# Keys of two groups in one turning DMA, x of the last two groups and z in fewer, heads a call later, and outputs stored behind the next load of u

## The chip, the cores and the metric

One core of a Trainium2 chip. The time is that of the whole kernel on the device, in microseconds; lower is better. Three runs of the kernel before gave 765.2, 765.59 and 769.08 us, median 765.59.

## The reference

Eight batches of 3200 tokens with 256 features. An attention without softmax, gated by `u`, gives `x`; a token mixer follows.

```python
scores = (1/S) * (z @ z.T)                # z: 3200 x 64, so scores are symmetric
x      = u * (maximum(scores, 0)**2 @ v)  # 3200 x 256
wq, wk = x @ w_q, x @ w_k                 # 3200 x 64 each
W_tok  = (1/8) * (wq @ wk.T)
out    = maximum(W_tok @ x, 0) @ w_out
```

The kernel never forms `W_tok`. It builds `wk.T @ x` (64 x 256, called the heads), multiplies that with `wq` (the mix), applies the maximum, and multiplies with `w_out` (the projection to the output).

## The kernel before

The 3200 tokens of a batch are 25 tiles of 128, in six groups of 512 and a last one of 128 (LASTG, the short group). Groups are worked off one after the other, batch after batch, in phases counted by `k`. The loop `while groups` (lines 1012 to 1215) writes out one phase per turn, and each engine gets its instructions in that written order; no planner reorders them.

A usual phase holds three pairs of score tiles (`scores`, L291) and a share of the second product (`acc`, L353) of the current group. A pair of score tiles is two matmuls that use 64 rows of TensorE each and run side by side, 512 columns long. The first stage takes the maximum (`g`, on DVE L305 or ACT L303), the second squares it (`at`, on POOL L316 or ACT L314). Two phases later `at` is the weight of the second product, with `v` as the moving side. Since the scores are symmetric, some `at` tiles are also turned by a DMA on SP's queue (`tt`, `ts`, L335) and serve a later group.

The second product is issued in two lanes: the upper 64 rows work on one bank of the accumulator and the lower 64 on the other (`first_pass`), then they change banks (`second_pass`). `swap_after` puts a wait for the first pass's last matmuls between them. Score pairs of the phase are placed at shares of it given by `shares_of` (L932), or, for the first `heading` of them (L1039 to L1045), ahead of everything:

```python
heading = len(pairs)
if on_lanes:
    heading = heading - 2 * bool(keying or projecting) if begins else 1 - bool(mixing)
```

So a phase that begins a group and holds neither a key call nor a projection has all its pairs ahead.

When a group closes, `gate` reads the two accumulator banks: DVE multiplies one with `u` (`x_sb`, L491), ACT copies the other (`gt`, L490) and POOL multiplies that (L493). The accumulator has one buffer per half, so the next group's first `acc` waits for both reads. `turn_x` turns x by a DMA (L502). Some phases later a key call (`keys_and_heads`, `k` below) projects a group: a matmul gives 64 rows of `wq` and 64 of `wk` in one PSUM tile `qk`. ACT copies all 128 rows to `qk` in SBUF (L528), and `turn_keys` turns the key half by a DMA (L535). The same call holds the heads of an earlier group, two key calls back, which DVE adds up (`ha`, L578). With the last group, DVE writes `hT` (L582) and TensorE turns it through the identity (`turn_heads`, L594). Then come six mix pieces a batch (`mix`, `m` below: two matmuls, one `rt` on ACT, and two score pairs instead of three) and six projections (`project`, `p` below: 16 `fo` matmuls, one ACT scaling L723, a store L724 on SP's queue at once). The short group's mix and projection ride along in key calls as side items.

Which phase holds a `k`, `m` or `p` is decided by rules (`mix_due`, `key_due`, `projecting`), with exceptions for 15 phases in `chosen` (L895). PSUM holds three two-bank tiles (`pps`), shared by scores, `qk`, `mx` and `fo`, and two accumulator banks. The last batch and the ending (a list of words, L82) are written out by hand.

Of the kernel before, what the change touches and what calls it, by code (L numbers as in the profile page):

```python
# [16 lines left out]
def kernel(  # L17
# [170 lines left out]
    zeros = consts.tile([P, P], FP16, tag="zeros", name="zeros")  # L188
    kxs = [pk.tile([P, 4, 2, dh], FP16, tag=f"kx{i}", name=f"kx{i}") for i in range(4)]
    raw = {}  # L190

# [27 lines left out]
    LASTG = NG - 1  # L219

    def is_turned(gi, gj):
        return gi < gj < LASTG and (gj <= gi + FAR or (gi, gj) == (0, 4))

    FOR_SMALL = (3, 4, 5)

# [244 lines left out]
    def gate(b, gi):  # L472
        nn = widths[gi] // P
        if gi < LASTG:
            xs[b, gi] = px.tile([P, 4, D], FP16, tag="x_sb", name="x_sb")
        else:
            xs[b, gi] = px.tile([P, 1, D], FP16, tag="xl", name="xl", bufs=1)
        x = xs[b, gi][:].rearrange("p n d -> p (n d)")
        ug = us.pop((b, gi))[:].rearrange("p n d -> p (n d)")
# [16 lines left out]
    def turn_x(b, gi):  # L496
        nn = widths[gi] // P
        if gi < LASTG:
            xTs[b, gi] = pxt.tile([P, 4, ND, P], FP16, tag="xT_sb", name="xT_sb")
        else:  # L500
            xTs[b, gi] = pxt.tile([P, 1, ND, P], FP16, tag="xTl", name="xTl", bufs=1)
        nc.sync.dma_start_transpose(  # L502
            out=xTs[b, gi][:, 0:nn, :, :].rearrange("p n a s -> p (n a) s"),
            in_=xs[b, gi][:, 0:nn, :].rearrange("p n d -> p (n d)"),
        )


# [14 lines left out]
    def projections_out(b, gi, out):  # L522
        gw = widths[gi]
        if gi < LASTG:
            qks[b, gi] = pq.tile([P, W], FP16, tag="qk", name="qk")
        else:
            qks[b, gi] = pq.tile([P, P], FP16, tag="ql", name="ql", bufs=2)
        nc.scalar.copy(out=qks[b, gi][:, 0:gw], in_=out)  # L528

    def turn_keys(b, gi):  # L530
        gw = widths[gi]
        mine = slice(0, dh) if swapped(gi) else slice(dh, P)
        kxs.append(kxs.pop(0))
        ks[b, gi] = kxs[-1]
# [170 lines left out]
    def proj_out(b, gi, src, ways):  # L705

        n0 = starts[gi] // P
        if groups:
            fo = pfo.tile([P, 2, W], FP32, tag="fo", name="fo")
        else:  # L710
            fo = pg.tile([P, 2, W], FP32, tag="g", name="fo")
        flat_out = fo[:].rearrange("p a w -> p (a w)")
        at = 0
        for on_dve, queue, n in ways:
            sl = slice(at * D, (at + n) * D)
            part = src[at // 2][:, 0 : n * D] if isinstance(src, list) else src[:, sl]
# [7 lines left out]
            queue.dma_start(  # L724
                out=rows(out, b)[:, n0 + at : n0 + at + n, :],
                in_=flat_out[:, sl].rearrange("p (n d) -> p n d", d=D),
            )
            at += n

# [34 lines left out]
    def side_proj_out(b, ps):  # L764
        fo = pfo.tile([P, D], FP32, tag="fs", name="fs", bufs=1)
        nc.scalar.mul(out=fo[:], in_=ps[:, 1, D : 2 * D], mul=FINAL_SCALE)
        nc.sync.dma_start(out=rows(out, b)[:, NT - 1, :], in_=fo[:])


    fillers = []  # L770
    to_load = []
    todo_mix, todo_proj, todo_between, at_phase, side = [], [], [], {}, []
    keyed, keyed_at, to_turn, to_spread, asides = [], [-9], [], [], []
    hTs, to_turn_heads = {}, []

# [6 lines left out]
    def group_done(k, b, gi):  # L782
        if gi < LASTG - 1:
            between(k + (5 if b + 1 < B else 3), lambda: keys_and_heads(b, [gi]))
        elif gi == LASTG and b + 1 < B:
# [11 lines left out]
    def keys_and_heads(b, gis):  # L797
# [5 lines left out]
        aside = None  # L803
        late = len(groups) <= NG
        heads_of = keyed[: late or len(keyed) == 2]
        if late and len(keyed) == 2 and keyed[0][0] == keyed[1][0]:
            heads_of = [(keyed[0][0], keyed[0][1] + keyed[1][1])]
            keyed[:2] = heads_of
        full = len(heads_of) == 1
        if full:  # L810
# [7 lines left out]
            if heads_of[0][0] < last and more < D:  # L818
# [5 lines left out]
                banks[1][-1].stop = False  # L824
                banks[1] += projections(b, gis[0], w, ps[:, 1, 0:P], start=False, n0=W // P - 1)
        assert full or len(gis) == 1
        if full and heads_of[0][0] < last and heads_of[0][1][-1] == LASTG:
# [4 lines left out]
        def after():  # L832
# [3 lines left out]
            if full:  # L836
                hb, hgis = keyed.pop(0)
                heads_out(hb, hgis, ps)
# [4 lines left out]
            if aside:  # L843
                aside[1](aside[2], ps)
            keyed.append((b, gis))
            keyed_at[0] = now[0]
# [3 lines left out]
    def group_begun(k, b, gi):  # L850
# [5 lines left out]
        if gi == 0 and b + 1 < B:  # L856
            for i, (n0, nn) in enumerate([(0, 16), (16, NT - 16)]):
                at = k + (5 if b == 0 else 1) + i
                due(at, lambda n0=n0, nn=nn: load_z(b + 1, n0, nn))
            for i, n0 in enumerate((0, 5, 9)):  # L860
                due(k + (10 if b == 0 else 6) + i, lambda n0=n0: turn_z(b + 1, n0, 5 if n0 == 0 else 4))
            n = NT // 2
# [149 lines left out]
    while groups:  # L1012
# [206 lines left out]

    assert not at_phase and not side and not todo_between   # L1220
    fillers = todo_proj + fillers
    assert not todo_mix and len(fillers) <= 3
# [8 lines left out]

    assert len(fillers) == 3 and all(kb == last for kb, _ in keyed)
    ps_, out_, g32 = {}, {}, {}
# [7 lines left out]
    def ending(order):  # L1241
        for word in order.split():
            what, n, more = word[0], int(word[1:2] or 0), word[2:]
            if what == "H":
                ps_["hd"] = ps_tile("hd")
                heads_ = heads(last, sum((kgis for _, kgis in keyed), []), ps_["hd"], stop=False)
                for fn in whole([heads_]):
# [90 lines left out]
```

## Time and profile before

| | |
|---|---|
| median of three runs | 765.59 us |
| the profiled execution, its time | 765.27 us |
| its span | 763.5 us |
| TensorE busy, share of the span | 753.3 us, 99% |
| DVE, ACT, POOL busy | 462.0, 526.4, 545.3 us |
| DMAs issued on SP's queue: `tt`, `ts`, `xT`, `kx`, `zT` | 162, 24, 48 + 8, 47 + 7, 21 |
| granted TensorE clock | 0.997 |

A row of the groups by line gives line, engine, operation, output and inputs with their shapes and the count; then busy time, mean length of one in ns, and the idle time of the engine ahead of it with what ended it. A row of the instructions in order of time gives start and length in us, engine, line, operation, and the count of equal neighbours merged into it. A wait row gives who waited for whom, the total in us, how often, and the longest. Lines are those of the kernel before.

### The profile page before, as it was taken

The page shows a single profiled execution, that of the slowest core. Times are in us where ns is not written, and L with a number is a line of the kernel's source. Part 1 is how long each engine was busy: PE and PEld are TensorE (multiplying, and loading weights), DVE is VectorE, ACT ScalarE, POOL GpSimd, SP SyncE. Part 2 cuts the span into 40 slices and gives each one's busy share as a digit, 9 for nine tenths or more (in the row PEclk, how much of TensorE's full clock was granted, in tenths as well). Part 3 has the DMA queues.
Part 4 walks back from the last instruction along what each step waited for, and adds up shares of the span by engine and source line. Part 5 has one row for each costly group of instructions (what it writes and reads, how often), then busy time and mean ns, then how long its engine had stood idle before and what let it go on. Part 6 is the DMA issues. An engine that isn't in the chain of part 4 may idle for free.

```text
span 763.5 us, 28995 instructions
## 1 busy us (share of the span) xinstructions
PE 753.3 (99%) x12888; PEld 617.9 (81%) x12888; DVE 462.0 (61%) x458; ACT 526.4 (69%) x619; POOL 545.3 (71%) x383
## 2 busy tenths in 40 slices
PE   8999999999999999999999999999999999999996
PEld 6777888888888887888888888888878888888884
DVE  7654676546755567555665557655566565755534
ACT  8666676676767676676775867658676586776555
POOL 7988797678867688675888569966698665854540
PEclk9999999999999999999999999999999999999998
DMA  9999699997999979999999979999599995798636
GB/s 193 176 191 201 104 175 175 141 181 112 183 172 205 188 146 187 201 189 171 191 195 194 210 151 150 169 201 237 105 198 204 200 209 127 170 227 188 168 74 261
DMA packets 289613, 135.88 MB, mean 178 GB/s; under 512 B 265168, under 2 KB 269648, under 8 KB 289488
## 3 DMA queue, kind: packets, MB, share of 16 engines
q1 hardware_dynamic: 279696, 117.80, 80.2%
q0 software_dynamic: 9648, 15.98, 15.3%
q8 instruction: 100, 1.64, 0.9%
q14 instruction: 25, 0.20, 0.1%
q10 hardware_dynamic: 144, 0.26, 0.1%
HBM read 59.38 MB, written 26.21 MB: 112 GB/s over the span
## 4 chain that ended last, share of the span: by engine, by line
PE 97%; DVE 2%; ACT 1%; issue 0%; DVEq 0%; ACTq 0%
PE acc L353 72%; PE sc L291 12%; PE fo L353 5%; PE qk L353 5%; PE mx L641 1%; DVE x_sb L491 1%; DVE fo L1296 0%; PE sc L965 0%; DVE g L305 0%; ACT at L314 0%; ACT g L303 0%; PE qk L594 0%; PE xtx L618 0%; PE ztp L129 0%; PE hd L628 0%
## 5 line engine op out<-in xcount | busy, mean ns | idle before, releaser
L305 DVE TENSOR_SCALAR g<-sc 128x1024 f32<-128x1024 f32 x329 | 400.6, 1224 | 240.2 <-PE sc L291 228.5
L316 POOL TENSOR_TENSOR at<-g 128x1024 f16<-128x1024 f32 x229 | 432.3, 1897 | 123.9 <-DVE g L305 100.2
L353 PE MATMUL acc<-v_sb,at 64*128 64x256 f16 (+1 forms) x7187 | 462.0, 269 | 2.2 <-DVE x_sb L491 0.5
L353 PEld LDWEIGHTS <-at 64*128 64x128 f16 (+1 forms) x7187 | 353.9, 94 | 87.6 <-PE acc L353 25.3
L314 ACT ACTIVATE at<-g 128x1024 f16<-128x1024 f32 x227 | 236.2, 1055 | 19.3 <-DVE g L305 11.8
L353 PE MATMUL acc<-v_sb,tt 64*128 64x256 f16 x2552 | 178.7, 269 | 0.0
L303 ACT ACTIVATE g<-sc 128x1024 f32<-128x1024 f32 x127 | 130.0, 1023 | 55.3 <-PE sc L291 52.3
L291 PE MATMUL sc<-zT 64*128 64x512 f16 (+1 forms) x1008 | 164.7, 356 | 0.4 <-DVE zT L135 0.3
L353 PEld LDWEIGHTS <-tt 64*128 64x128 f16 x2552 | 130.2, 94 | 14.1
L493 POOL TENSOR_TENSOR x_sb<-gt,u_sb 128x512 f16<-128x512 f32 x48 | 61.2, 1274 | 64.5 <-ACT gt L490 60.1
L662 ACT ACTIVATE rt<-mx 128x1024 f16<-128x1024 f32 x47 | 47.9, 1024 | 32.7 <-PE mx L641 32.5
L490 ACT COPY gt<-acc 128x512 f32<-128x512 f32 x48 | 28.1, 585 | 49.9 <-PE acc L353 49.9
L291 PEld LDWEIGHTS <-zT 64*128 64x128 f16 x1008 | 51.8, 94 | 8.7 <-issue 1.5
L353 PE MATMUL fo<-wo,rt 64*128 64x256 f16 (+1 forms) x696 | 57.9, 270 | 0.0
L528 ACT CAST qk<-qk 128x512 f16<-128x512 f32 x47 | 27.5, 586 | 39.5 <-PE qk L353 36.9
L353 PEld LDWEIGHTS <-rt 64*128 64x128 f16 (+1 forms) x696 | 35.5, 94 | 15.3 <-PE fo L353 6.3
L491 DVE TENSOR_TENSOR x_sb<-acc,u_sb 128x512 f16<-128x512 f32 x48 | 33.2, 691 | 20.4 <-PE acc L353 19.2
L723 ACT ACTIVATE fo<-fo 128x1024 f32<-128x1024 f32 x39 | 39.9, 1024 | 1.9 <-PE fo L353 1.7
L353 PEld LDWEIGHTS <-x_sb 64*128 64x128 f16 x672 | 29.8, 95 | 4.5 <-PE qk L353 0.9
L353 PE MATMUL qk<-kx,x_sb 64*128 64x64 f16 x672 | 32.8, 190 | 0.0
L146 POOL DMA_DIRECT2D v_sb<-in_v_dram x49 | 28.7, 586 | 0.0
L353 PE MATMUL qk<-xT_sb,wkq 64*128 64x512 f16 (+3 forms) x118 | 25.7, 326 | 0.0
(84 smaller groups left out, 249.8 us busy)
## 6 DMA issues: line engine op xcount, KB each, us to landing
u_sb<-in_u_dram SPq DMA_DIRECT2D x48, 512.0 KB, 5.4
out_dram<-fo SPq DMA_DIRECT2D x43, 512.0 KB, 3.9
v_sb<-in_v_dram POOLq DMA_DIRECT2D x43, 256.0 KB, 5.2
tt<-at SPq DMA_TRANSPOSE x162, 5.1
out_dram<-fo SPq DMA_DIRECT2D x9, 256.0 KB, 2.9
zr<-in_z_dram POOLq DMA_DIRECT2D x7, 256.0 KB, 4.2
u_sb<-in_u_dram SPq DMA_DIRECT2D x8, 128.0 KB, 4.4
zr<-in_z_dram POOLq DMA_DIRECT2D x7, 144.0 KB, 6.4
```

The source lines that it names most:

```text
L146: nc.gpsimd.dma_start(out=vs[b][:, n0 : n0 + nn, :], in_=rows(v, b)[:, n0 : n0 + nn, :])
L291: nc.tensor.matmul(out=sc[:, h, at : at + w], lhsT=zT[b][half : half + dqk, ds(z_at(b, h) + ti * P, P)], rhs=zT[b][half : half + dqk, ds(z ...
L303: nc.scalar.activation(out=g[:], in_=sc[:], func=RELU, scale=GSCALE)
L305: nc.vector.tensor_scalar(out=g[:], in0=sc[:], scalar1=0.0, scalar2=GSCALE, op0=AOP.max, op1=AOP.mult)
L314: nc.scalar.square(out=out, in_=g[:])
L316: nc.gpsimd.tensor_mul(out=out, in0=g[:], in1=g[:])
L353: return nc.tensor.matmul(out=self.out, lhsT=self.lhsT(rows), rhs=self.rhs(rows), start=start, stop=stop)
L490: nc.scalar.copy(out=upper[:], in_=accs[1][:])
L491: nc.vector.tensor_mul(out=x[:, 0:n], in0=accs[0][:, 0:n], in1=ug[:, 0:n])
L493: nc.gpsimd.tensor_mul(out=x[:, n : 2 * n], in0=upper[:], in1=ug[:, n : 2 * n])
L662: nc.scalar.activation(out=out, in_=ps[:], func=RELU)
L723: nc.scalar.mul(out=flat_out[:, sl], in_=part, mul=FINAL_SCALE)
```

## The change

Keys: the key half of a group's `qk` now goes through a DVE copy into a tile `kp` that holds two groups, one in each 64 rows, and a single DMA turns both (with the short group's 128 columns added for the last pair). ACT copies only the other half, into a tile that two groups share. x: the short group's x lies in the same tile as that of group 5, and one DMA turns both when the short group closes. z is turned in two pieces instead of three. The heads of a group come at least two key calls after its pair was turned. Stores of outputs are put on a list that is emptied behind the next load of `u`, or ahead of the next output. EXTRAS now fixes for every phase whether it holds a key call, a mix piece or a projection (`x`: mix and projection). The last batch keeps the old way with its keys. Pools change in size.

```diff
-    px = ctx.enter_context(tc.tile_pool(name="px", bufs=7))
+    px = ctx.enter_context(tc.tile_pool(name="px", bufs=6))
-    pxt = ctx.enter_context(tc.tile_pool(name="pxt", bufs=4))
+    pxt = ctx.enter_context(tc.tile_pool(name="pxt", bufs=3))
-    pq = ctx.enter_context(tc.tile_pool(name="pq", bufs=11))
+    pq = ctx.enter_context(tc.tile_pool(name="pq", bufs=6))
...
+        elif gi == LASTG - 1:
+            xs[b, gi] = px.tile([P, 5, D], FP16, tag="x5", name="x5", bufs=2)
+        else:
+            xs[b, gi] = xs[b, gi - 1][:, 4:5, :]
...
+            if gi == LASTG - 1:
+                xTs[b, gi] = pxt.tile([P, 5, ND, P], FP16, tag="xT5", name="xT5", bufs=1)
+                xTs[b, LASTG] = xTs[b, gi][:, 4:5, :, :]
+            if b < last:
+                if gi < LASTG:
+                    return
+                n0, n1 = 0, 5
...
+        q, k = (slice(dh, P), slice(0, dh)) if swapped(gi) else (slice(0, dh), slice(dh, P))
+        nc.scalar.copy(out=qks[b, gi][q, :], in_=out[q, :])
+        nc.vector.tensor_copy(out=kps[b, pair][k, 0:W], in_=out[k, :])
...
+        kx = pk.tile([P, 5, 2, dh], FP16, tag="kp2", name="kx", bufs=2)
         nc.sync.dma_start_transpose(
-            out=ks[b, gi][:, 0 : gw // P, 0, :],
-            in_=qks[b, gi][mine, 0:gw],
+            out=kx[:, 0:n, :, :].rearrange("p n a h -> p n (a h)"), in_=kps[b, pair][:, 0 : n * P]
         )
...
-            queue.dma_start(
+            store = lambda at=at, n=n, sl=sl, queue=queue: queue.dma_start(
...
+            if groups:
+                each(to_store)
+                to_store[:] = [store]
...
-        late = len(groups) <= NG
-        heads_of = keyed[: late or len(keyed) == 2]
...
+        ready = [x for x in keyed if calls[0] - x[2] >= (1 if b == last else 2)]
...
-            for i, n0 in enumerate((0, 5, 9)):
+            for i, (n0, nn) in enumerate(((0, 7), (7, 6))):
...
-    heading_more = {165: -1}
-    chosen = {
-        18: "k", 19: "p", 20: "p", 21: "m", 35: "k", 36: "p", 38: "p", 101: "p", 142: "mp",
-        147: "k", 148: "m", 149: "m", 159: "mp", 161: "p", 163: "m"
-    }
+    heading_more = {}
+    EXTRAS = (
+        ".............k..k..k..k..k..k...k..k..k...mk..km.km.kmpk.ppkmpmkmpkmppkmp.km"
+        "mpk.mkppkmmkpmmpk.pkmmk.pkpmmkppkpmkm.kp.kmpkpmkmppkmmkpmpmkmpkpxkm.kppkpm.k"
+        "mmkxpkxxkxxkm.pk."
+    )
+    chosen = {k: "mp" if c == "x" else c for k, c in enumerate(EXTRAS)}
...
             load_u(*to_load.pop(0))
+            while to_store:
+                to_store.pop(0)()
```

More of the change, by code (lines that the diff above doesn't have):

```diff
@@ L188 @@
     zeros = consts.tile([P, P], FP16, tag="zeros", name="zeros")
-    kxs = [pk.tile([P, 4, 2, dh], FP16, tag=f"kx{i}", name=f"kx{i}") for i in range(4)]
-    raw = {}
+    kxs = [pk.tile([P, 4, 2, dh], FP16, tag=f"kx{i}", name=f"kx{i}") for i in range(2)]
+    raw, kps = {}, {}
     def load_weights():
@@ L727, in proj_out @@
             )
+            if groups:
+                each(to_store)
+                to_store[:] = [store]
+            else:
+                store()
             at += n
@@ L766, in side_proj_out @@
         nc.scalar.mul(out=fo[:], in_=ps[:, 1, D : 2 * D], mul=FINAL_SCALE)
-        nc.sync.dma_start(out=rows(out, b)[:, NT - 1, :], in_=fo[:])
+        to_store.append(lambda: nc.sync.dma_start(out=rows(out, b)[:, NT - 1, :], in_=fo[:]))
     fillers = []
-    to_load = []
+    to_load, to_store = [], []
     todo_mix, todo_proj, todo_between, at_phase, side = [], [], [], {}, []
     keyed, keyed_at, to_turn, to_spread, asides = [], [-9], [], [], []
-    hTs, to_turn_heads = {}, []
+    hTs, to_turn_heads, calls = {}, [], [0]
     def due(k, fn):
@@ L783, in group_done @@
         if gi < LASTG - 1:
-            between(k + (5 if b + 1 < B else 3), lambda: keys_and_heads(b, [gi]))
+            between(
+                k + (5 if b < last else 2 if gi == LASTG - 2 else 3), lambda: keys_and_heads(b, [gi])
+            )
         elif gi == LASTG and b + 1 < B:
@@ L803, in keys_and_heads @@
         aside = None
-        late = len(groups) <= NG
-        heads_of = keyed[: late or len(keyed) == 2]
-        if late and len(keyed) == 2 and keyed[0][0] == keyed[1][0]:
-            heads_of = [(keyed[0][0], keyed[0][1] + keyed[1][1])]
-            keyed[:2] = heads_of
+        ready = [x for x in keyed if calls[0] - x[2] >= (1 if b == last else 2)]
+        if b >= last - 1 and len(ready) > 1 and ready[0][0] == ready[1][0]:
+            keyed[:2] = [(ready[0][0], ready[0][1] + ready[1][1], ready[1][2])]
+            ready = keyed[:1]
+        heads_of = [x[:2] for x in ready[:1]]
         full = len(heads_of) == 1
@@ L825, in keys_and_heads @@
                 banks[1] += projections(b, gis[0], w, ps[:, 1, 0:P], start=False, n0=W // P - 1)
+        elif side and len(gis) == 1:
+            aside = side.pop(0)
+            banks[1] += aside[0](aside[2], ps)
+            banks[1][0].start = True
         assert full or len(gis) == 1
@@ L844, in after @@
                 aside[1](aside[2], ps)
-            keyed.append((b, gis))
+            if b == last:
+                keyed.append((b, gis, calls[0]))
+            elif gis[0] % 2 == 1:
+                keyed.append((b, [gis[0] - 1], calls[0]))
+                keyed.append((b, gis, calls[0]))
+            calls[0] += 1
             keyed_at[0] = now[0]
@@ L1220 @@
     assert not at_phase and not side and not todo_between
+    each(to_store)
     fillers = todo_proj + fillers
@@ L1228 @@
         turn_x(*to_turn.pop(0))
-    assert len(fillers) == 3 and all(kb == last for kb, _ in keyed)
+    assert len(fillers) == 3 and all(x[0] == last for x in keyed)
     ps_, out_, g32 = {}, {}, {}
@@ L1245, in ending @@
                 ps_["hd"] = ps_tile("hd")
-                heads_ = heads(last, sum((kgis for _, kgis in keyed), []), ps_["hd"], stop=False)
+                heads_ = heads(last, sum((x[1] for x in keyed), []), ps_["hd"], stop=False)
                 for fn in whole([heads_]):
```

65 lines of the change are left out of this document (47 added, 18 removed).

## The prediction

> **What bounds the kernel now.** I read the page's busy shares first, then its chain, then the groups by line, and last the instructions in order of time around a few points where the work changes from one group of 512 tokens to the next.
>
> ```profile
> span 763.5 us, 28995 instructions
> PE 753.3 (99%) x12888; PEld 617.9 (81%) x12888; DVE 462.0 (61%) x458; ACT 526.4 (69%) x619; POOL 545.3 (71%) x383
> ...
> PE 97%; DVE 2%; ACT 1%; issue 0%; DVEq 0%; ACTq 0%
> ...
> L305 DVE TENSOR_SCALAR g<-sc 128x1024 f32<-128x1024 f32 x329 | 400.6, 1224 | 240.2 <-PE sc L291 228.5
> ...
> L353 PE MATMUL acc<-v_sb,at 64*128 64x256 f16 (+1 forms) x7187 | 462.0, 269 | 2.2 <-DVE x_sb L491 0.5
> ```
>
> TensorE is on 97% of the chain, and the other engines idle a third of the time. "99% busy" hides small gaps, because each matmul's row is 269 ns long while the next pair starts earlier. The step between pairs has to be taken from starts, in the order of time below (start, length, engine, line, count). A bare beginning of a group, in the phase from 163.23 to 168.37:
>
> ```profile
> 163.23 0.82 PE L291 MATMUL sc<-zT 64*128 64x512 f16 x12
> 163.43 0.59 ACT L490 COPY gt<-acc 128x512 f32<-128x512 f32 x1 [1.44 <-PE acc L353]
> 163.47 0.69 DVE L491 TENSOR_TENSOR x_sb<-acc,u_sb 128x512 f16<-128x512 f32 x1 [1.37 <-PE acc L353]
> ...
> 164.07 1.83 PE L353 MATMUL acc<-v_sb,at 64*128 64x256 f16 x28
> ...
> 165.65 0.69 PE L353 MATMUL acc<-v_sb,tt 64*128 64x256 f16 x8
> ...
> 166.39 1.70 PE L353 MATMUL acc<-v_sb,at 64*128 64x256 f16 x28
> ...
> 167.93 0.60 PE L353 MATMUL acc<-v_sb,tt 64*128 64x256 f16 x8
> ...
> 168.37 0.60 PE L291 MATMUL sc<-zT 64*128 64x128 f16 x10
> ```
>
> And a beginning with a projection (`fo`) in it, from 318.22 to 323.72:
>
> ```profile
> 318.22 0.38 PE L291 MATMUL sc<-zT 64*128 64x512 f16 x2
> ...
> 318.44 0.60 PE L353 MATMUL fo<-wo,rt 64*128 64x256 f16 x8
> ...
> 318.87 0.38 PE L291 MATMUL sc<-zT 64*128 64x512 f16 x2
> ...
> 319.10 0.61 PE L353 MATMUL fo<-wo,rt 64*128 64x256 f16 x8
> ...
> 319.55 1.69 PE L353 MATMUL acc<-v_sb,at 64*128 64x256 f16 x28
> ...
> 321.51 0.38 PE L291 MATMUL sc<-zT 64*128 64x512 f16 x2
> ...
> 321.74 1.70 PE L353 MATMUL acc<-v_sb,at 64*128 64x256 f16 x28
> ...
> 323.72 0.59 PE L291 MATMUL sc<-zT 64*128 64x512 f16 x4
> ```
>
> Units: two score matmuls (the two row halves side by side) step 318.22 to 318.44, 0.218 us for 512 columns; so a pair of 256 columns is 0.109 us (8 `fo`, four pairs, 318.44 to 318.87). The second phase holds 6 scores, 16 `fo`, 72 `acc`: 0.65 + 0.87 + 3.92 = 5.45 us; it took 5.50, so 0.05 is lost. The first holds scores of the same columns and 72 `acc`: 0.65 + 3.92 = 4.57; it took 5.14, so 0.56 is lost, in two places. At 164.07 `acc` waits for the group's last accumulator to be read out (ACT until 164.02, DVE until 164.16), since 0.65 us of scores don't cover that. At 166.39, where the halves change banks, nothing stands between the two passes of `acc`; in the other phase a score pair does (321.51) and the second pass follows it at once. Two more bare beginnings, the latter after the short group of 128 tokens, whose read-out is shorter:
>
> ```profile
> 36.90 0.81 PE L291 MATMUL sc<-zT 64*128 64x512 f16 x6
> ...
> 42.03 0.38 PE L291 MATMUL sc<-zT 64*128 64x512 f16 x2
> ```
>
> ```profile
> 460.48 0.83 PE L291 MATMUL sc<-zT 64*128 64x512 f16 x6
> 461.16 3.48 PE L353 MATMUL acc<-v_sb,at 64*128 64x256 f16 x56
> 464.48 0.59 PE L291 MATMUL sc<-zT 64*128 64x512 f16 x4
> ```
>
> 5.13 against 4.57 (72 `acc` again), 0.56 lost; and 4.00 against 0.65 + 3.05, 0.30 lost: there the change of banks is nearly all of it.
>
> **The change part by part.** The sum is made against the profiled execution's own 765.27 us (span 763.5 and 1.8 around it), 0.3 below the median 765.59.
>
> *TensorE's work.* Counted over the built order of both kernels, columns times halves are the same: 737.6 us at the unit above. 40 fewer matmuls come from a few phases issued with all 128 rows instead of in halves. Worth 0.
>
> *Where the extras stand.* The table EXTRAS replaces the rules that gave most beginnings a projection or a key call. In the built order of before, a long run of `acc` with no score inside, behind a full group, begins 3 groups (36.90 and 163.23 are two). In the order after, it begins 17: ten with three score pairs ahead, seven with one `mx` pair and two score pairs, again 0.65 us of cover. The projections go to the middle of groups, where they cost their columns only. So 14 beginnings change from 0.05 to 0.56 lost: 14 x 0.51 = +7.1 us. Bounds: if read-outs are covered and only the bank change stays, 14 x 0.25 = +3.5 (from 460.48); if the read-out also comes late, more:
>
> ```profile
> ACT gt L490 <- PE acc L353: 49.9, 43, 3.1
> ...
> DVE x_sb L491 <- PE acc L353: 19.2, 34, 1.4
> ```
>
> In 14 of 48 closings DVE came to `x_sb` late, not idle. If that holds at the bare ones, behind a first stage (L305's 1.22 us), 14 x 14/48 x 1.22 = 5.0 more: +12.1. I take 7.1, as all three early beginnings behind full groups were on time. The short groups' own beginnings lose 0.3 in both orders.
>
> *Keys of two groups in one transpose.* Each of 42 key calls gets a DVE copy of 64x512 out of PSUM, seven also one of 128x128. In the built order that copy waits for ACT's copy of the same tile, and the heads' addition comes behind it. Such a call in before, where the heads are also turned on TensorE:
>
> ```profile
> 326.38 1.23 DVE L305 TENSOR_SCALAR g<-sc 128x1024 f32<-128x1024 f32 x1 [0.95 <-PE sc L291]
> ...
> 327.07 0.59 ACT L528 CAST qk<-qk 128x512 f16<-128x512 f32 x1 [0.69 <-PE qk L353]
> ...
> 327.69 0.49 DVE L582 TENSOR_TENSOR hT<-ha,qk 128x128 f16<-128x128 f32 x2
> 327.71 1.04 PE L353 MATMUL acc<-v_sb,tt 64*128 64x256 f16 x16
> 328.68 0.11 PEld L594 LDWEIGHTS <-hT 128*128 128x128 f16 x2 [0.21 <-issue]
> ```
>
> The new copy reads 512 fp32 columns from PSUM on DVE, as x_sb's 0.69 us does, and I take that. 42 x 0.69 + 7 x 0.3 = 31 us on an engine that is 61% busy: nothing in itself. But `hT` would end at 328.18 + 0.69 + 0.03 = 328.90, 0.22 behind 328.68 where TensorE now loads it. Five of the seven turnings keep this cover (1.74 us of matmuls between the call's last write and the turning), one has 2.61, the last batch's has no copy: 5 x 0.22 = +1.1, bounds 0 and 5 x 0.69 = 3.5. The Trainium skill, PSUM — Partial Sum Buffer, section PSUM bank collisions raise a hardware error, lets two engines into one bank at the same time if they are in different quadrants of partitions; ACT and DVE now read different halves, so by it the copies could run side by side, and this term and the next would be 0, the sum 772.4. The trace speaks against that here: the DVE instruction behind ACT's copy starts 0.03 after its end.
>
> The same chain sets the PSUM tile free:
>
> ```profile
> L578 DVE TENSOR_TENSOR ha<-ha,qk 128x128 f32<-128x128 f32 x27 | 7.7, 286 | 8.7 <-ACT qk L528 4.9 <-ACT ql L528 3.6
> ...
> L528 ACT CAST ql<-qk 128x128 f16<-128x128 f32 x7 | 1.9, 271 | 0.0
> ...
> L747 ACT ACTIVATE rs<-qk 128x256 f16<-128x256 f32 x7 | 2.7, 384 | 3.1 <-DVE ha L576 3.1
> ```
>
> Some 0.3 us from the start of the call's last write, then 0.59 + 0.03 + 0.69 + 0.03 + 0.29, together 1.9; 0.6 more with the short group in it (`ql` and its copy), 0.4 more with `rs` behind. In the order after, TensorE's work up to the next write to those banks is longer in all calls but six, which are short by 0.1 to 0.5, 1.5 in all: +1.5. Bounds: 0, and +9.7 if one more first stage (1.22) stands ahead on DVE in each of the eleven calls with under 3 us of such work.
>
> *Fewer and longer transposes.* 42 fewer instructions on SP's queue, with the same bytes: keys 54 to 26, x 56 to 49, z 21 to 14; group 5's x waits for the short group, one phase of some 4 us, and is read five phases after that.
>
> ```profile
> ACT at L314 <- DMA tt<-at: 5.1, 4, 2.7
> ...
> POOL at L316 <- DMA tt<-at: 3.8, 4, 1.3
> ```
>
> No TensorE wait names a DMA; what transposes delay is ACT and POOL, 8.9 us in all, under first stages that themselves wait 228 us for TensorE. I take 0; bounds -8.9 (all of it passed on) and 0. The Trainium skill, DMA: Bandwidth & Descriptors, section Anatomy of one DMA, gives each GpSimd-issued DMA a fixed cost of about 2 us; carried over as an estimate, 42 fewer are 84 us of transfers' waiting, and by it the change would gain wherever one is waited for (rival C). No run shows one that TensorE waits for.
>
> *Stores behind the next load of u.* SP no longer stands waiting for `fo` ahead of later transposes; same queue, same cover, 0. The output tile (two of them) is stored a phase or two later, with no third projection due before the first has left. *Heads a call later*: one more x tile is held, and the six plus two suffice. *Eight second stages* go from POOL to ACT: both idle about 30%. All 0; without that cover, they would cost at most a second stage each.
>
> Sum: 765.3 + 7.1 + 1.1 + 1.5 = 775.0, forecast **775 us**.
>
> **The rivals.** *A, only the bank change is paid.* If the read-out at a beginning is hidden (the `mx` pair and quieter ACT and DVE let the group's tile go sooner), 14 x 0.25 = 3.5, and no turning waits: 768.8, not slower by the bound used here, 0.5% or 3.8 us, about what a measurement of this kernel tells from no change. It decides below 0.27 lost per bare beginning. For it: 460.48. Against: 36.90 and 163.23, the same form as the new ones.
>
> *B, DVE holds the banks.* The copy behind ACT's copy comes late in the key calls: 765.3 + 7.1 + 1.1 + 9.7 = 783. For it: at 326.38 a first stage ends just before the chain. Against: DVE waits 228 us for scores.
>
> *C, the queue was the bound.* Fewer transposes pass their 8.9 us on and beginnings stay covered: 756. For it: ACT's and POOL's waits above. Against: TensorE's chain of 97%, its equal work, and what a phase with extras loses, 0.05.
>
> **How the numbers follow.** The forecast (770 to 780) has 0.62, A 0.13, B 0.16, C 0.04, and 0.05 goes to no change because parts that I took as 0 repay the losses. Slower by over 0.5% (above 769.4) are the forecast, B and the upper quarter of A: 0.81; within 0.5% the rest of A and the repaid case: 0.15; faster C: 0.04. The range takes in A's 768.8 and B's 783; the forecast alone would be 770 to 780.
>
> **What would show it.** In the trace after, TensorE's order of time should hold a run of `acc` x72 broken by 0.2 to 0.4 us in its middle and delayed at its start, at about 17 beginnings, each some 0.5 us over its columns. `kp` on DVE should take about 0.69 and start just behind ACT's `qk`; the turning's weight load should wait for `hT` for 0.2. SP's waits for `fo` should be gone with no TensorE gain. The prediction fails if bare beginnings lose under 0.3, if `kp` starts together with ACT's copy, or if gaps before scores appear in key calls.

## The result

The changed kernel is slower: 787.74 us median (784.65 to 791.5), before 765.65 in the same comparison, ratio 1.0281 with a 95% interval of 1.0222 to 1.0339. The profiled execution took 789.5 us with a span of 787.4, so 23.9 more than the span of before. The forecast was 775, with a range that takes in 768.8 and 783: the sign was right, the size too small, and the measured time lies above the range. Ratios leave out executions over 1.5% slower than the fastest of their kernel; of the runs below that touches one, in which two of four took 805.4 and 812.09 us.

Spans are of one execution each. Those of the changed kernel's four lie between 782.5 and 789.7, so a difference of two spans is good to a few us only; smaller terms are read from the phases, which are introduced below.

The head of the page, busy groups, and the waits of the changed kernel (who waited for whom, total in us, how often, longest; line numbers are from here on those of each run's own kernel):

```profile
span 787.4 us, 28826 instructions
PE 764.1 (97%) x12848; PEld 625.1 (79%) x12848; DVE 487.3 (62%) x505; ACT 535.0 (68%) x626; POOL 529.1 (67%) x373
```

```profile
L557 DVE CAST kp<-qk 64x512 f16<-64x512 f32 x42 | 28.9, 687 | 25.2 <-ACT qk L556 24.3
```

```profile
DVE kp L557 <- ACT qk L556: 24.3, 14, 3.8
POOL at L318 <- DMA tt<-at: 21.2, 6, 4.9
ACT at L316 <- DMA tt<-at: 17.0, 6, 4.9
ACT fo L766 <- DMA out_dram<-fo: 6.1, 5, 2.2
PE sc L293 <- ACT g L305: 3.7, 3, 2.1
PEld L637 <- DVE hT L625: 3.1, 6, 0.8
PE sc L293 <- DVE ha L621: 2.6, 3, 1.4
```

The new DVE copy takes the 0.69 us that was forecast, and DVE is at 62%. But 14 times DVE stands idle at the head of its queue with this copy, 24.3 us in all; the waits for turnings of `at` rose from 8.9 us to 38.2; and scores now wait for `ha` and for ACT's first stage; before has no such row. A bare beginning (instructions in order of time) looks as the forecast drew it, with the delayed start (0.24 us behind its scores at 170.81) and 0.3 us lost between the passes (the first has 18 pairs of 0.109, which end at 172.77; the second starts at 173.08):

```profile
169.92 0.82 PE L293 MATMUL sc<-zT 64*128 64x512 f16 x12
170.81 1.77 PE L355 MATMUL acc<-v_sb,at 64*128 64x256 f16 x28
172.34 0.69 PE L355 MATMUL acc<-v_sb,tt 64*128 64x256 f16 x8
173.08 1.70 PE L355 MATMUL acc<-v_sb,at 64*128 64x256 f16 x28
174.62 0.60 PE L355 MATMUL acc<-v_sb,tt 64*128 64x256 f16 x8
175.06 0.33 PE L293 MATMUL sc<-zT 64*128 64x128 f16 x6
```

It takes 5.14 us against 4.57 of columns, 0.56 lost, the number of the prediction. What the forecast didn't have is this, around the key call before the beginning at 112.44:

```profile
107.94 7.26 SPq L337 DMA_TRANSPOSE tt<-at  x4
...
110.42 1.06 ACT L316 ACTIVATE at<-g 128x1024 f16<-128x1024 f32 x1 [4.86 <-DMA tt<-at]
111.38 1.00 ACT L305 ACTIVATE g<-sc 128x1024 f32<-128x1024 f32 x1
112.29 0.56 ACT L556 CAST qk<-qk 64x512 f16<-64x512 f32 x1
112.44 0.61 PE L293 MATMUL sc<-zT 64*128 64x512 f16 x4 [2.09 <-ACT g L305]
...
112.89 0.69 DVE L557 CAST kp<-qk 64x512 f16<-64x512 f32 x1 [2.83 <-ACT qk L556]
...
113.59 0.29 DVE L621 TENSOR_TENSOR ha<-ha,qk 128x128 f32<-128x128 f32 x1
113.80 0.68 DVE L495 TENSOR_TENSOR x_sb<-acc,u_sb 128x512 f16<-128x512 f32 x1
...
113.94 0.39 PE L293 MATMUL sc<-zT 64*128 64x512 f16 x2 [0.89 <-DVE ha L621]
...
114.54 0.82 PE L355 MATMUL acc<-v_sb,at 64*128 64x256 f16 x6 [0.21 <-DVE x_sb L495]
```

Read it downwards. ACT waits 4.86 us with a second stage, because its buffer `at` is still being turned by a DMA that SP issued late. Behind that stage stand a first stage and the copy of `qk`, which ends at 112.85. DVE has put `kp` at the head of its queue and does nothing for 2.83 us. Scores wait 2.09 us for the tile that ACT's first stage holds, then 0.89 more for the tile that `ha` holds, and `x_sb` is so late that the accumulator isn't free.

The stop costs more than its length. TensorE stood still from 110.35 to 112.44 and in part up to 114.54, and from 114.36 on its granted clock was 0.50 for 3.41 us (window; busy time and count of PE, PEld, DVE, ACT and POOL; granted clock, DMA share, GB/s):

```profile
112.00:114.36 2.36, 1.00 (x6) 0.22 (x6) 1.46 (x3) 2.36 (x5) 0.95 (x1) 1.00 1.21 268
114.36:117.77 3.41, 3.23 (x32) 2.69 (x33) 2.38 (x3) 2.73 (x3) 3.06 (x3) 0.50 1.02 195
```

Half the clock over 3.23 us of busy TensorE is some 1.6 us, an estimate from these rows. Neither the kernel before nor the one with 13 tiles below has such a stretch ahead of its last 5 us.

To see where all of the 23.9 us went I took each phase's time, from its first matmul to the next phase's in the built order, and took off its columns at the unit of the prediction (0.218 us for 512 columns on both halves). The columns are equal in all kernels here. What is left, summed over the phases, is 12.5 us before and 36.7 after. The phases that stand out are used below.

### The profile page after: what moved, and what is told of

It is laid out like the page before. It is cut to its first block, busy times and chain, and to the rows that moved or that the text cites. A ratio compares the mean times of both kernels' runs of the same rounds, so it can differ in the third digit from the quotient of the medians.

```text
span 787.4 us, 28826 instructions
## 1 busy us (share of the span) xinstructions
PE 764.1 (97%) x12848; PEld 625.1 (79%) x12848; DVE 487.3 (62%) x505; ACT 535.0 (68%) x626; POOL 529.1 (67%) x373
## 5 line engine op out<-in xcount | busy, mean ns | idle before, releaser
L318 POOL TENSOR_TENSOR at<-g 128x1024 f16<-128x1024 f32 x221 | 416.9, 1895 | 144.7 <-DVE g L307 111.8
L355 PEld LDWEIGHTS <-at 64*128 64x128 f16 (+1 forms) x7187 | 360.5, 94 | 88.5 <-PE acc L355 24.4
L316 ACT ACTIVATE at<-g 128x1024 f16<-128x1024 f32 x235 | 243.8, 1054 | 31.4 <-DMA tt<-at 17.0
L355 PE MATMUL acc<-v_sb,tt 64*128 64x256 f16 (+1 forms) x2536 | 181.0, 269 | 0.0
L355 PEld LDWEIGHTS <-tt 64*128 64x128 f16 (+1 forms) x2536 | 131.1, 94 | 13.6
L497 POOL TENSOR_TENSOR x_sb<-gt,u_sb 128x512 f16<-128x512 f32 x40 | 50.9, 1273 | 59.2 <-ACT gt L494 58.3
L293 PEld LDWEIGHTS <-zT 64*128 64x128 f16 x1008 | 53.0, 94 | 24.4 <-issue 10.4
L557 DVE CAST kp<-qk 64x512 f16<-64x512 f32 x42 | 28.9, 687 | 25.2 <-ACT qk L556 24.3
L556 ACT CAST qk<-qk 64x512 f16<-64x512 f32 x42 | 24.2, 577 | 28.1 <-PE qk L355 27.9
L495 DVE TENSOR_TENSOR x_sb<-acc,u_sb 128x512 f16<-128x512 f32 x40 | 27.6, 690 | 17.8 <-PE acc L355 17.1
L355 PEld LDWEIGHTS <-x_sb 64*128 64x128 f16 x560 | 24.4, 95 | 4.7 <-PE qk L355 0.6
L355 PE MATMUL qk<-kx,x_sb 64*128 64x64 f16 x560 | 27.0, 190 | 0.2 <-ACT fo L766 0.2
```

Of the source, the lines that this page charges most:

```text
L293: nc.tensor.matmul(out=sc[:, h, at : at + w], lhsT=zT[b][half : half + dqk, ds(z_at(b, h) + ti * P, P)], rhs=zT[b][half : half + dqk, ds(z ...
L316: nc.scalar.square(out=out, in_=g[:])
L318: nc.gpsimd.tensor_mul(out=out, in0=g[:], in1=g[:])
L355: return nc.tensor.matmul(out=self.out, lhsT=self.lhsT(rows), rhs=self.rhs(rows), start=start, stop=stop)
L497: nc.gpsimd.tensor_mul(out=x[:, n : 2 * n], in0=upper[:], in1=ug[:, n : 2 * n])
L557: nc.vector.tensor_copy(out=kps[b, pair][k, 0:W], in_=out[k, :])
```

## The experiments

**The table alone, and everything but the table.** The first kernel is before with EXTRAS:

```diff
-    heading_more = {165: -1}
-    chosen = {18: "k", 19: "p", ...}
+    heading_more = {}
+    EXTRAS = (
...
+    chosen = {k: "mp" if c == "x" else c for k, c in enumerate(EXTRAS)}
```

> The kernel before with the new table EXTRAS alone: same keys, x, z, stores. Theory P (places): where key calls, mix pieces and projections stand makes most of the +22 us, by bare beginnings (+7.1) and by key calls that now stand in a group's beginning and hold a PSUM tile there; this run then takes 780 to 788. Theory K (keys and queue): the DVE copy of the keys and late transposes make the rest; then this run pays the bare beginnings alone, 771 to 775.

777.52 us, ratio 1.0128 (1.0047 to 1.021), span 772.6, that is 9.1 above before. By phases it loses 20.9 us, 8.4 more. Its 14 new bare beginnings lose 0.54 to 0.66 each, 8.0 in all, where the same groups' beginnings of before lost 0.8: 7.2 more. Another 1.0 us is lost in phase 78, where the heads are turned on TensorE: ACT is late by a second stage that waited for a turning of `at`, so its copy of `qk` and with it `hT` come late.

```profile
347.01 1.06 ACT L314 ACTIVATE at<-g 128x1024 f16<-128x1024 f32 x1 [2.35 <-DMA tt<-at]
...
350.43 0.48 DVE L582 TENSOR_TENSOR hT<-ha,qk 128x128 f16<-128x128 f32 x2 [0.96 <-ACT qk L528]
...
350.97 0.28 PE L594 MATMUL qk<-ident,hT 128*128 128x128 f16 x2 [0.77 <-DVE hT L582]
```

The time lies between the two ranges, and its interval is wide and reaches into both; the phases speak for K. The second is the changed kernel with the same edit reversed:

> The changed kernel with the old rules for the places: new keys, x, z and stores stay. Theory P: back to 765 to 770. Theory K: 776 to 782, the loss of some 13 to 15 us beside the bare beginnings stays. Both could be needed at once: then this run and the table alone each lose little, under 8, and only together 22.

774.74, ratio 1.0108 (1.0073 to 1.0142), span 773.0. That is above theory P's 770 and just under theory K's 776. The new keys, x, z and stores cost by themselves, with the old places too. With the table they cost 14.8 us of span (772.6 to 787.4), without it 9.5 (763.5 to 773.0).

**Bare beginnings alone.** Before, with one rule changed so that projections stand behind a beginning, not in it:

```diff
-            else begins or len(todo_proj) > 2 or len(groups) <= NG
+            else not begins or len(groups) <= NG
```

> The kernel before, in which a projection no longer stands in the phase that begins a group but in the phases after it (one word of the rule; keys, x, z and stores as before). That makes 17 more bare beginnings behind full groups and three behind short ones. By my first step, 17 x 0.51 + 3 x 0.25 = 9.4 us more, 774 to 777, without any of the new keys. Rival: bare beginnings are dear only beside the new keys and late turnings; 766 to 770.

775.31, ratio 1.0139 (1.0107 to 1.0172), span 773.0: 9.5 more, for 9.4 worked out. The new bare beginnings behind full groups lose 0.54 to 0.71 each. This step of the prediction stands, in another arrangement and with the old keys.

**Merged x and z, and more tiles in the kernel before.** The first takes the new `turn_x`, the tile of five for x and the two pieces of z into the kernel before; the second changes one number.

```diff
-            for i, n0 in enumerate((0, 5, 9)):
+            for i, (n0, nn) in enumerate(((0, 7), (7, 6))):
```

> The kernel before with x of the last two groups in one turning and z in two pieces, nothing else. My step took it as free: 765 to 767.5. Rival: the longer turnings make those of at late and cost by themselves, 769 to 772.

765.68, ratio 0.999 (0.9977 to 1.0004). Free, and worth nothing.

```diff
-    NAT = 11
+    NAT = 13
```

> The kernel before with 13 tiles for at. Its ACT and POOL wait 8.9 us for turnings; if these are covered, as the forecast took them, no change, 764.5 to 767. If they are passed on, up to 4 us faster than before, 761 to 764.

766.66, ratio 1.0007 (0.9996 to 1.0018). The 8.9 us of waits for turnings in before were covered, as the prediction took them.

**13 tiles for at in the changed kernel.** The same edit.

> The changed kernel with 13 tiles for at instead of 11, so that a second stage need not wait for the turning of an older at. ACT and POOL wait 38 us for these turnings now, against 9 before. If these waits are passed on to TensorE, as the trace suggests at 112, 359, 428 and 495 us, 5 to 10 us faster than the changed kernel (778 to 783); if they are covered, no change, 786 to 789.

782.43, ratio 1.0182 (1.0114 to 1.025), span 780.8, 6.6 under the changed kernel; each of its four executions (781.29 to 782.93) was faster than each of the changed kernel's. The waits nearly vanish:

```profile
POOL at L318 <- DMA tt<-at: 1.8, 2, 1.6
```

The late turnings weren't covered in the changed kernel. Some 1.6 of the 6.6 us is the stretch at half the clock, which is gone with the stop at 110.35. Yet the table alone has as many late turnings and loses little by them: of its 20.9 us, 12.5 are lost before too, 7.2 are the new beginnings and 1.0 is phase 78. Its wait rows are

```profile
POOL at L316 <- DMA tt<-at: 24.8, 9, 4.5
ACT at L314 <- DMA tt<-at: 16.1, 10, 3.2
```

those of everything but the table, the changed kernel with the old places, are

```profile
POOL at L318 <- DMA tt<-at: 25.1, 10, 4.3
ACT at L316 <- DMA tt<-at: 9.1, 8, 1.9
```

so each half of the change makes turnings late by itself. This is the table alone in its key call at the place of the lump above, where ACT also waited for a turning:

```profile
106.94 1.06 ACT L314 ACTIVATE at<-g 128x1024 f16<-128x1024 f32 x1 [1.64 <-DMA tt<-at]
107.90 1.01 ACT L303 ACTIVATE g<-sc 128x1024 f32<-128x1024 f32 x1
...
108.56 1.23 DVE L305 TENSOR_SCALAR g<-sc 128x1024 f32<-128x1024 f32 x1 [0.86 <-PE qk L353]
108.84 0.58 ACT L528 CAST qk<-qk 128x512 f16<-128x512 f32 x1
109.70 0.28 DVE L578 TENSOR_TENSOR ha<-ha,qk 128x128 f32<-128x128 f32 x1
109.92 0.81 PE L291 MATMUL sc<-zT 64*128 64x512 f16 x6
```

There ACT was late by less, and no copy stood between `qk` and `ha`; this pair of traces doesn't tell which of the two counts.

**Stores at once.** The changed kernel without `to_store`.

```diff
-            if groups:
-                each(to_store)
-                to_store[:] = [store]
-            else:
-                store()
+            store()
```

> The changed kernel with outputs stored at once, as before. If the held-back stores keep the two output tiles (ACT waited 6.1 us for them in 5 places), 2 to 5 us faster than the changed kernel (783 to 786); if SP's standing at the stores costs as much, or the waits are covered, 787 to 789.

783.58, ratio 1.0207 (1.0138 to 1.0277), span 784.6, 2.8 less. The waits for `fo`'s store are gone, and those for turnings of `at` fell from 38.2 to 21.9 us, but the intervals of the two kernels overlap; that held-back stores cost is likely, not shown.

**The key copy out of SBUF.** ACT copies all 128 rows out of PSUM, as before, and DVE fills `kp` from that copy, behind `ha`:

```diff
-        nc.scalar.copy(out=qks[b, gi][q, :], in_=out[q, :])
-        nc.vector.tensor_copy(out=kps[b, pair][k, 0:W], in_=out[k, :])
+        nc.scalar.copy(out=qks[b, gi][:], in_=out)
...
+        nc.vector.tensor_copy(out=kps[b, gi // 2][k, 0:W], in_=qks[b, gi][k, :])
```

> The changed kernel, but ACT copies all 128 rows of the key call's product out of PSUM as before, and DVE fills kp from that copy in SBUF, behind the heads' addition. The one DMA for two groups, the table, x, z and the stores stay. Theory D: the DVE copy in the chain that sets the PSUM tile free makes most of what the table alone doesn't explain; its phases lose 1.2 (twice), 1.0, 0.8 (twice), 0.7 and several times 0.4 to 0.5 us more than with the table alone, so 8 to 10 us faster, 777 to 781. Rival Q: the late turnings of at (nearly all of the rest) make them; then 783 to 788.

785.65, ratio 1.0255 (1.0222 to 1.0288). With 13 tiles too:

> The same with 13 tiles for at. If the PSUM tile (D) and the late turnings of at (Q) together are all beside the table, it comes to what the table alone took, 774 to 778. If a third thing is in it (x of two groups at once, held-back stores), 779 or more.

782.95, ratio 1.022 (1.0199 to 1.0241), no faster than 13 tiles alone. Theory D was missed both times, and the first time came out where rival Q has it. But the phases show that D was half right: the two dear turnings (phases 81 and 120) fell from 0.84 lost to 0.23, phases 29 and 112 from 1.05 to 0.56. In return phases 56, 106 and 115, which had lost 0.1 at most, lose 0.9 to 1.0. The lines of the two copies, DVE's here and ACT's in the kernel further below (duration in ns: least, median, most):

```profile
L563 DVE COPY kp<-qk x42: 274/804/2858, 53.8 to 687.8; 64x512 f16<-64x512 f16 x42
```

```profile
L563 ACT COPY kp<-qk x42: 615/616/620, 54.3 to 679.2; 64x512 f16<-64x512 f16 x42
```

The DVE copy is held up, by up to 2.6 us. One of the long ones, with all of DVE's and POOL's instructions around it:

```profile
244.46 1.91 POOL L318 TENSOR_TENSOR at<-g 128x1024 f16<-128x1024 f32 x1
245.92 0.29 DVE L627 TENSOR_TENSOR ha<-ha,qk 128x128 f32<-128x128 f32 x1 [1.95 <-ACT qk L554]
246.12 2.86 DVE L563 COPY kp<-qk 64x512 f16<-64x512 f16 x1
246.30 0.59 POOL L146 DMA_DIRECT2D v_sb<-in_v_dram  x1
246.91 1.91 POOL L318 TENSOR_TENSOR at<-g 128x1024 f16<-128x1024 f32 x1
248.90 1.21 DVE L307 TENSOR_SCALAR g<-sc 128x1024 f32<-128x1024 f32 x1
```

So this run replaced one wait by another and couldn't decide between D and Q; the copy had to go to another engine.

**Heads as early as before.** My next theory was that phases 66, 87, 109 and 148 lose by the later heads, since they lose the same with the copy out of SBUF.

```diff
-        ready = [x for x in keyed if calls[0] - x[2] >= (1 if b == last else 2)]
-        if b >= last - 1 and len(ready) > 1 and ready[0][0] == ready[1][0]:
+        ready = [x for x in keyed if calls[0] - x[2] >= 1]
+        if b == last and len(ready) > 1 and ready[0][0] == ready[1][0]:
```

> The changed kernel with the heads of a group held by key calls as early as before (one call behind its pair's turning, not two). With them the short group's side items go back to the calls that held them with the table alone. Theory H: four phases (66, 87, 109, 148) lose 1.2, 1.1, 1.4 and 0.7 us more than with the table alone because a side item in a key call that begins a group puts two score pairs ahead of it and the third finds no PSUM tile; without it 4 us faster than the changed kernel, 782 to 785. Rival: those phases wait for the DVE copy, 786 to 789.

799.95, ratio 1.0448 (1.0423 to 1.0473): 12 us slower than the changed kernel, where I expected 4 faster. With 13 tiles:

> The same with 13 tiles for at, so without the turnings' lateness. H: 4 us under the 782.4 of 13 tiles alone, 777 to 780. Rival: 781 to 784.

801.83, ratio 1.0479 (1.0446 to 1.0512). TensorE now waits for the keys; the rows of the first of the two, and one of its waits:

```profile
PE qk L355 <- DMA kx<-kp: 16.5, 5, 5.4
PEld L355 <- DMA kx<-kp: 16.1, 4, 5.8
```

```profile
392.63 1.34 SPq L575 DMA_TRANSPOSE kx<-kp  x1
...
396.93 0.10 PEld L355 LDWEIGHTS <-x_sb 64*128 64x128 f16 x1 [5.75 <-DMA kx<-kp]
396.94 0.23 PE L355 MATMUL qk<-kx,x_sb 64*128 64x64 f16 x1 [5.37 <-DMA kx<-kp]
```

One turning for two groups can't start before the second group's keys are there, and then takes 4.3 us from issue (392.63) to use. In this order of calls "heads a call later" is no separate choice; it is what the one DMA requires. The waits aren't the whole price, either. Each of the three longest leaves TensorE at half its clock: the granted clock is 0.50 for 6.83 us from 395.30, 432.84 and 501.11, beginning within the wait, and 24 `acc` matmuls that take 1.47 us at full clock (changed kernel, 108.88) take 2.77 at 398.62. TensorE is busy for 16.5 of these 20.5 us, so the clock costs some 8.2 us, an estimate, of the 25.5 that the five phases with these waits lose. Two more kernels were built on the same early heads: 13 tiles and the key copy moved to ACT (below), once with the table, once with the old rules.

> Heads as early as before, 13 tiles for at, and the keys copied by ACT from SBUF into kp (ACT first copies all 128 rows out of PSUM, as before), so that neither DVE nor the PSUM tile is held by the second copy. The table, the one DMA for two groups, x, z and the stores stay. If heads, tiles for at and the copy's chain are all that there is beside the table, 774 to 778, as with the table alone (777.5). If ACT's added copies (42 of some 0.6 us) or the held-back stores cost, 779 to 783.

799.75, ratio 1.0452 (1.0408 to 1.0496).

> The same with the old rules for the places of key calls, mix pieces and projections. If the table's bare beginnings are the rest, 765 to 768, no slower than before; if the new keys cost by themselves still, 769 to 774.

Ratio 1.0318 (1.0297 to 1.0339), span 787.4. All four expectations on early heads were missed, by 10 us and more. The last two kernels lose their time in the few phases that wait for `kx`, 1.8 to 8.0 us each, and have stretches at half the clock as well. Outside of them the first loses in phases 29, 79, 81, 112, 120 and 148 what the table alone loses there, to 0.01 us. So the pieces were named rightly there, but the totals could not show it.

**The copy on ACT, heads late as in the changed kernel.**

```diff
-        nc.vector.tensor_copy(out=kps[b, pair][k, 0:W], in_=out[k, :])
...
+        nc.scalar.copy(out=kps[b, gi // 2][k, 0:W], in_=qks[b, gi][k, :])
...
-    NAT = 11
+    NAT = 13
```

> The changed kernel with 13 tiles for at and ACT copying all 128 rows out of PSUM, then the key half from SBUF into kp; heads as late as in the changed kernel. Turnings (81, 120, 38, 101, 138) and the phases 26, 29, 70, 112 should lose what they lose with the table alone, 4.5 us less than with 13 tiles alone: 777 to 779.5. What stays beside the table is the side items' new calls (66, 87, 148), some 3 us. Rival: a copy in SBUF is no cheaper on ACT than it was on DVE; 781 to 784.

777.97, ratio 1.0161 (1.0146 to 1.0176), span 775.9: as theory D had it, 4.9 under 13 tiles alone. With 11 tiles, the copy's edit alone:

> The changed kernel with the key copy on ACT, out of SBUF, as in the run that took 778, but with 11 tiles for at as in the changed kernel. If late turnings of at reach TensorE by themselves (ACT waits, its first stages and copies come late), their 6 us come back: 783 to 786. If they reach it only where DVE's key copy stands behind ACT's late copy, nearly nothing comes back: 777.5 to 780.

780.86, ratio 1.0207 (1.0173 to 1.024), span 778.0, between the two. The tiles are worth 2.1 us of span now and 6.6 with the DVE copy, so late turnings reach TensorE without that copy too, but at a third of the price. How much of the difference is the copy is not shown: with ACT's copy the turnings are also less late (waits of 18.7 us in all, 38.2 in the changed kernel), and no stretch runs at half the clock.

**One score pair ahead.** In phases 66 and 87 a key call begins the group and holds the short group's side item, and then the code puts two score pairs ahead of it, not one. In the changed kernel, at phase 66:

```profile
295.66 0.59 PE L293 MATMUL sc<-zT 64*128 64x512 f16 x4
...
295.95 0.58 ACT L494 COPY gt<-acc 128x512 f32<-128x512 f32 x1
...
296.43 1.03 ACT L305 ACTIVATE g<-sc 128x1024 f32<-128x1024 f32 x1
...
297.51 0.39 PE L293 MATMUL sc<-zT 64*128 64x512 f16 x2 [0.80 <-ACT g L305]
```

Two score tiles and `qk` fill the three PSUM tiles, and the third pair waits until ACT, which had `gt` first, has read one.

```diff
-    heading_more = {}
+    heading_more = {66: -1, 87: -1}
```

> The same, with one score pair ahead instead of two in the phases 66 and 87, which begin a group with a key call and a side item in it. If the third pair's missing PSUM tile is what costs there, each loses 0.1 instead of 1.2, 2.3 us less than the run before; if it is the key call itself, no less.

Phases 66 and 87 lose 0.08 and 0.07 instead of 1.24 and 1.16, as expected. Phase 70 gives 1.06 of it back. The span is 774.0, 1.9 less; the times (779.41 median, 775.79 to 784.63) scatter too much to tell it.

**All repairs, with the old rules.** 13 tiles, the copy on ACT, stores at once, the old places.

> New keys in one turning for two groups, x and z merged, heads a call later; but 13 tiles for at, the key copy on ACT, stores at once, and the old rules for the places. If the table, the tiles for at, the copy's chain and the stores were all, 765 to 768, as before; each phase over that is the later heads, whose side items fall into other calls: 768 to 772.

768.19, ratio 1.0046 (1.0027 to 1.0064), span 766.4. Nearly back, and 2.9 us of span remain. Phases 40, 59, 62 and 67 hold it: they lose 0.62, 0.77, 1.00 and 0.76, and 0.29, 0.03, 0.06 and 0.02 both before and with early heads and the old rules. The changed kernel with the old places loses 0.9 us and more in each of them, with stores held back. So it is the later heads' price in this arrangement. No version was faster than the kernel before.

The losses of the phases that tell the repairs apart, in us over their columns (worked out as said above; "+ copy" is 13 tiles and ACT's copy, "+ one pair" the run after it):

| phase | before | table alone | changed | 13 tiles | + copy | + one pair |
|---|---|---|---|---|---|---|
| 25, 26 key call, bare beginning | 0.11 | 0.57 | 5.53 | 1.17 | 0.57 | 0.57 |
| 79 bare beginning | 0.05 | 0.62 | 2.20 | 0.56 | 0.56 | 0.56 |
| 81, 120 turnings of hT | 0.05 | 0.04 | 1.68 | 1.68 | 0.46 | 0.46 |
| 29, 112 bare beginnings | 0.12 | 1.12 | 2.10 | 2.10 | 1.12 | 1.12 |
| 66, 87 side item in a beginning | 0.18 | 0.17 | 2.45 | 2.45 | 2.40 | 0.15 |
| 70 | 0.05 | 0.09 | 0.48 | 1.09 | 0.09 | 1.15 |
| all phases | 12.5 | 20.9 | 36.7 | 30.3 | 24.4 | 22.8 |

## Why the prediction was wrong

By spans, the 23.9 us are 9.1 for the table (772.6 less 763.5), 3.3 more for late heads with x, z, stores and the key copy on ACT, at 13 tiles (775.9), 4.9 for that copy on DVE in place of ACT (780.8) and 6.6 for the late turnings (787.4), with some 1.6 of half clock in it. The last two depend on the order in which they are taken off, as the run with ACT's copy and 11 tiles shows (9.4 for the copy first, 2.1 for the tiles then).

*Where the extras stand*, 7.1: right, in mechanism, place and size. 7.2 over the 14 beginnings with the table alone, and 9.5 for 9.4 in the arrangement made to test it. What it lacked of the table's cost is the turning that comes late in phase 78, 1.0. Rival A (only the change of banks is paid) is out.

*Keys of two groups in one transpose*, 1.1 + 1.5: the mechanism was right and the size wrong. `kp` takes 0.69 us and starts 0.04 behind ACT's copy, and `hT` is late. But the turnings lost 0.61 (twice), 0.24 (twice) and 0.16 by it, 1.9 in all by what ACT's copy gives back, where 1.1 was forecast: the cover that the step gave them was gone, since four of the five lose 0.2 with ACT's copy too. Of the rest of the 4.9, 1.0 is phase 70 and isn't the copy's: with 13 tiles alone, ACT waits 2.0 us there for `fo`'s store and TensorE 0.9 for ACT's `fo`. The others are mostly phases 26, 29, 112 and 148. That the PSUM tile held longer costs them is argued from such waits as those of scores for `ha` (0.3 to 0.4 in 26 and 29), not tried by itself. The gaps before scores in key calls, which the prediction named as a sign that it fails, came. The bound of 9.7 supposed one more first stage ahead on DVE. What came was another thing: DVE stood still with `kp` at the head of its queue, behind ACT's late copy. This is rival B's place, DVE holding the banks, with the cause on ACT. As to the rule of the Trainium skill, PSUM — Partial Sum Buffer, section PSUM bank collisions raise a hardware error: a wait in the program sets the copies behind each other, so no run here tests whether they could run at once.

*Fewer and longer transposes*, 0 with bounds of -8.9 and 0: this is the step that failed worst. For x and z alone it holds (0.999). For the kernel before, that the waits are covered holds too (13 tiles: 1.0007). But I bounded the term by the waits that before had, as if they could only shrink. They grew to 38.2 us, and in the changed kernel they were no longer covered: 6.6 with the copy on DVE, 2.1 with ACT's and half the lateness. What makes the turnings late stays open. The table alone raises the waits as far (40.9 us in the two rows), but so does the rest of the change without the table (34.2); x and z alone hardly do (11.7).

*Heads a call later*, 0: failed. I looked whether the x tiles suffice, and not at what else hangs on the call: the side items of the short group move with the heads into calls that begin a group. That costs 1.1 us each in phases 66 and 87, shown by the run with one pair ahead (1.0 of it came back in phase 70); 0.8 in phase 109 and 0.7 in phase 110 also stay with ACT's copy and 13 tiles. In 109 scores wait 0.7 for ACT's `fs`; in 110 they wait 0.6 for ACT's `fo`, and ACT waits 2.7 for `fo`'s store, so 110 is the stores'. Neither was tried by itself.

*Stores behind the next load of u*, 0: "no third projection due before the first has left" is refuted by the row of ACT waiting 6.1 us for `fo`'s store, 5 times, where before has none. Phases 70 and 110 above show single places where that reaches TensorE; the whole price, 2.8 us of span, isn't separated from the scatter. *Eight second stages* weren't tried alone.

Rival C, that the queue was the bound, is out: fewer transposes gained nothing in any run. The four terms that I costed apart are not independent: new keys cost 9.5 with the old places and 14.8 with the new, which a sum of terms, each with its own cover, can't give. The likely reason is that they use the same cover, the few microseconds between a key call's last write and the next need of a PSUM tile.

## What to carry to other kernels

Where an edit puts an instruction between two engines' work on one PSUM tile, price not only its length but what its engine is made to wait for at the head of its queue: 42 copies of 0.69 us on a DVE at 62% cost some 4 to 5 us against the same copies on ACT, and some 9 where ACT's stages came late, because DVE and the tile then stood still with it. A wait that is covered before the change bounds nothing after it; ask for each cover whether the same edit uses it up. Where TensorE stands still, look at the granted clock behind it too: the stop can cost more than its length. When work of two groups is merged into one transfer, look for everything that is tied to the moment when its result is used, here the heads, and with them the side items.

## What the hardware showed that was not expected

The DVE copy of 64x512 from SBUF to SBUF in fp16 took 274 to 293 ns in the 16 of 42 cases that began with no POOL instruction running, and 291 to 2858 in the 26 that began during one; the same data out of PSUM in fp32 took a steady 0.69 us, and ACT's copy in SBUF a steady 0.62. The Trainium skill, SBUF — State Buffer, section SBUF: two separate sides, says that GpSimd and a DVE instruction in a two-port mode share one pair of ports, held for a whole instruction while the other fully blocks. The trace agrees: all 26 copies that began during a POOL instruction ended 0.14 to 0.17 us behind the end of one of POOL's multiplies. Three of them stood through two, such as the one that began at 246.12 and ended at 248.98, 0.16 us behind the end of the second (246.91 + 1.91). Why it didn't run in the 0.55 us between the two, in which POOL issued a DMA, isn't shown.

The granted clock fell to 0.50 where TensorE had stood still, for 3.41 or 6.83 us. The changed kernel has one such stretch ahead of its ending, worth some 1.6 us, as has the one with stores at once; each of the four kernels with early heads has three or four. It did not follow every stop: one of 2.09 us at 110.35 in the changed kernel had it, one of 2.66 at 107.18 in the first kernel with early heads had not.
